# Giving the normalising transposes a stretch of their own, with the scores ahead of the maxima behind it

## The chip, the cores and the metric

The kernel runs on one core of one Trainium2 chip. The metric is the device time of one execution in microseconds (us); the time before is the median of three runs. Everything that is read out of a profile comes from one profiled execution, whose own time stands beside it.

## What is computed

A sequence of 2048 rows of 640 numbers passes through four residual layers, A, B, A, B. Each layer first normalises its input rows. A is a linear attention block, B an attention block over four segments of 512 rows with a causal softmax inside a segment and a memory that carries over from the segments before. Both have 32 heads of 20 columns. Cut to what matters:

```python
def _A_ref(x, wqkv, wo):
    q, k, v = split_heads(x @ wqkv)
    phi = lambda t: jnp.where(t > 0, t + 1, jnp.exp(t)) + 1e-6
    pq, pk = phi(q), phi(k)
    kv = einsum("bhsd,bhse->bhde", pk, v)
    o = (pq @ kv) / (pq . sum(pk))
    return merge(o) @ wo

def _B_ref(x, wq, wk, wv, wo, beta):
    for s in range(4):
        logits = einsum("bhqd,bhkd->bhqk", qs, ks) * scale + causal_mask
        a_dot = softmax(logits) @ vs
        a_mem = (phi(qs) @ M) / (phi(qs) . z)
        o = g * a_mem + (1 - g) * a_dot
        M, z = M + phi(ks)^T vs, z + sum(phi(ks))
    return merge(o) @ wo

x = x + _A_ref(_layernorm(x), A...)
x = x + _B_ref(_layernorm(x), B...)
x = x + _A_ref(_layernorm(x), A...)
x = x + _B_ref(_layernorm(x), B...)
```

The change touches only the softmax part of B: scores, their row maxima, the exponentials, the weighted sum and the division by the sum.

## The kernel before, in words

Two generators write the program. One (`dense`, line 893) issues all projections, transposes and memory reads; the other (`attention`, line 799) issues the softmax part of B. `run` (line 972) interleaves them: each step of a generator returns a cost in nanoseconds, and the generator whose running cost is lower goes next (the dense costs are first divided by a rate that depends on the phase). TensorE (PE) executes in exactly the order in which the program is written. For the other engines a scheduler decides the order when the program is built, and it also decides which of the eight PSUM banks each result gets: all PSUM results share one pool of eight banks (`bank`, line 137), and a matmul that opens a bank waits until the engine that reads the bank's previous content is done.

The softmax part works on groups: a group is four heads of one segment, 8 groups to a segment, 32 to a B layer, 64 in all. A group has a pair index p (0, 1), a parity (0, 1) and row blocks of 128. Three groups are in flight, called new, prev and old, and one pass over a group's turn is a cycle. The operations of a cycle stand in the table `STRETCHES` (line 54), cut into three stretches; after each stretch `attention` gives up its turn at a cost of `SLOT` = 2420 (line 836), so that dense work goes between the stretches. An entry is an operation, an index and the group that it is for (0 new, 1 prev, 2 old):

- `max` (`row_max`, line 692): scores of query rows against keys, four or six matmuls (line 701) into two banks; VectorE (DVE) reads each bank with a masked maximum (line 708). Entries 0 to 3 have six matmuls or a pair of 512 columns with it, entry 4 has four of 256 columns.
- `split` and `rows` (lines 712 and 722): the maxima are split into two halves on DVE (lines 717 and 718), turned by one transpose on PE (line 726), copied by ScalarE (ACT, line 728) and sent by DMA into two rows of the query tile (line 731), so that the next score matmul subtracts the maximum itself.
- `exp` (`scores`, line 734): transposed scores, matmuls at line 743; each bank is read by one exponential on ACT (line 747), and GpSimd (POOL) clears what the mask excludes (line 754). Entries 0 and 1 open four banks in all, entries 2 and 3 four, entry 4 two.
- `sum` (`weigh`, line 762): the weighted sum, 16 matmuls (line 770; the profile counts 32 rows, since each runs as two) into one bank.
- `copy` (`evacuate`, line 774): ACT copies that bank to SBUF as `oTf` (line 776).
- `out` (`normalize`, line 778): the normalising transposes, four on PE from `oTf` into one bank (line 783); DVE takes the reciprocals of the sums (`rc`, line 786) and multiplies (line 790 for a first segment, otherwise `tmp`, line 793); POOL adds `tmp` to the output (line 794).

Before, a cycle on PE was therefore: scores of entry 4, maxima 0 and 1, the row transpose, the weighted sum, the copy on ACT; dense work; the transposes, maxima 2 and 3, scores 0 and 1; dense work; scores 2 and 3, maximum 4; dense work. The middle stretch opened nine banks: one for the transposes, four for maxima, four for scores.

A dense piece is 15 matmuls into one bank (line 337 with 320 columns or line 323 with 512; the latter is written as 9 and 6 around a turn), two or three transposes (line 280), three matmuls of a memory read (line 382), or four transposes or matmuls of the memory update (lines 589 and 597). Its bank is read by ACT (line 360, 404, 561, 349, 351 or 284) or by DVE.

Of the kernel before, what the change touches and what calls it, by code (L numbers as in the profile page):

```python
# [38 lines left out]
VW = H * E1 + 11  # L39
HB = H // 2  # L40
COL = 1 / 2.4
SLOT = 2420.0
R_SECOND, R_PROJ, R_MID, R_END = 2.2, 1.0, 1.2, 0.85


# [5 lines left out]
EXPS += [[((0, a, 2, 0), (1, a, 2, 256)) for a in range(2)]]  # L51


STRETCHES = [[("exp", 4, 2), ("max", 0, 0), ("max", 1, 0), ("rows", 0, 1), ("sum", 0, 2), ("sum", 1, 2), ("sum", 3, 2),
              ("sum", 2, 2), ("copy", 0, 2)],
             [("out", 0, 2), ("max", 2, 0), ("max", 3, 0), ("exp", 0, 1), ("exp", 1, 1)],
             [("exp", 2, 1), ("exp", 3, 1), ("max", 4, 0), ("split", 0, 0), ("load", 0, 0)]]


def constants():  # L60
# [64 lines left out]
class Kernel:  # L125
# [673 lines left out]
    def attention(self, segs):  # L799

        prev = old = ahead = None
        n = 0
        while n < NSEG * NG or prev or old:
            new = None
            if n < NSEG * NG:
                st = segs[n // NG]
                if not st.get("projected"):
                    yield lambda: st.get("projected")
                new = ahead or self.stacks(st, n % NG)
                ahead = None  # L810
            n += 1
            for stretch in STRETCHES:
                for op, k, back in stretch:
                    G = (new, prev, old)[back]
                    if op == "load" and n < NSEG * NG and segs[n // NG].get("projected"):
                        ahead = self.stacks(segs[n // NG], n % NG)
                    if G is None:
                        continue
                    if op == "max":
                        self.row_max(G, MAXES[k])  # L820
                    elif op == "split":
                        self.split_max(G)
                    elif op == "rows":
                        self.max_rows(G)
                    elif op == "exp":
                        for bank in EXPS[k]:
                            self.scores(G, bank)
                    elif op == "sum":
                        self.weigh(G, k)
                    elif op == "copy":  # L830
                        self.evacuate(G)
                    elif op == "out":
                        if not G["st"].get("remembered"):
                            yield lambda: G["st"].get("remembered")
                        self.normalize(G)
                yield SLOT
            old, prev = prev, new


# [188 lines left out]
```

## Time and profile before

| | us |
|---|---|
| median of three runs | 1817.21 (1815.69 to 1820.99) |
| the profiled execution | 1820.7 |
| its span, first to last instruction | 1818.9 |
| PE busy in the span | 1716.8 (94%) |
| DVE busy | 1112.6 (61%) |
| ACT busy | 940.2 (52%) |
| POOL busy | 549.1 (30%) |

A line of the profile names the source line, the engine, the operation and the tiles (`out<-in`), with how many instructions it holds; times are in us, means in ns. PEld is the loading of weights, which runs beside the matmuls. `<-` in a wait names what ended the idle time. The table of waits has the total, the number of waits and the longest. The timeline merges neighbouring instructions of one kind into a row: start, length, engine and line, and in square brackets the idle time ahead of it. The matmuls are pipelined and their ends are modelled, so the length of a row of matmuls runs on past the start of the next.

### The profile page before, as it was taken

Reading aid. Unit: us, or ns where it says so; the run is one execution under the profiler, and the core shown is the slowest. Engines: PE = TensorE matmul, PEld = TensorE weight load, DVE = VectorE, ACT = ScalarE, POOL = GpSimd, SP = SyncE. Lnnn points to the kernel's source line nnn. Section 1 sums busy time; section 2 is a strip of 40 time slices with the busy share of each in tenths; the row PEclk is TensorE's granted clock in tenths of the full one; section 3 lists DMA queues with packets and bytes.
Section 4 is the critical chain, followed back from the end, with each engine's and each line's share of the span. In section 5 each row is a group of like instructions: output and inputs, shape, how many; then the busy total and the mean of one; then the engine's idle time right before and its main releaser. Section 6 shows DMA issues by size and latency. Waiting matters only on the chain.

```text
span 1818.9 us, 36252 instructions
## 1 busy us (share of the span) xinstructions
PE 1716.8 (94%) x13032; PEld 1068.9 (59%) x13032; DVE 1112.6 (61%) x3729; ACT 940.2 (52%) x1753; POOL 549.1 (30%) x981
## 2 busy tenths in 40 slices
PE   6999999999999999998989999999999999999998
PEld 4666676654665565453556776756546546644555
DVE  7655443677777677766662321527677777777773
ACT  5455433266556546655564433223664664565664
POOL 1534440022123213324355334200221231232442
PEclk9999999999999999999999999999999999999999
DMA  7443343312212332352212112433122223223332
GB/s 256 155 166 116 147 144 100 122 53 93 94 63 85 109 100 72 109 195 66 72 56 89 51 34 91 138 100 101 50 92 90 92 85 103 96 77 107 127 109 88
DMA packets 123371, 185.96 MB, mean 102 GB/s; under 512 B 13740, under 2 KB 85548, under 8 KB 121016
## 3 DMA queue, kind: packets, MB, share of 16 engines
q1 hardware_dynamic: 109480, 137.44, 23.5%
q0 software_dynamic: 4496, 25.23, 3.8%
q10 hardware_dynamic: 9216, 20.98, 2.9%
q8 instruction: 103, 1.69, 0.4%
q14 instruction: 76, 0.62, 0.1%
HBM read 104.41 MB, written 78.64 MB: 101 GB/s over the span
## 4 chain that ended last, share of the span: by engine, by line
PE 75%; DVE 11%; ACT 5%; issue 4%; POOL 2%; DMA 2%; SPq 1%; ACTq 0%; POOLq 0%; DVEq 0%
PE ps L337 32%; PE ps L323 18%; PE ps L770 7%; DVE junk L708 4%; PE ps L743 3%; PE ps L280 3%; PE ps L382 3%; ACT pe L747 2%; PE ps L701 2%; PE ps L467 2%; PE ps L597 1%; POOL e L353 1%; PE ps L783 1%; DVE st L298 1%; DMA qs<-mt 1%
## 5 line engine op out<-in xcount | busy, mean ns | idle before, releaser
L708 DVE CUSTOM_DVE_ANT_0 junk<-ps,maskw 128x512 bf16<-128x512 f32 (+3 forms) x1024 | 499.5, 488 | 90.2 <-PE ps L701 28.7
L747 ACT ACTIVATE pe<-ps,lsc 128x512 f32<-128x512 f32 x640 | 391.7, 691 | 124.0 <-PE ps L743 116.9
L754 POOL TENSOR_SCALAR_AFFINE_SELECT pe<-pe 128x256 f32<-128x256 f32 (+1 forms) x640 | 232.0, 369 | 426.3 <-ACT pe L747 420.1
L337 PEld LDWEIGHTS <-xT 128*128 128x128 f16 x2880 | 281.5, 99 | 123.1 <-issue 9.2
L337 PEld LDWEIGHTS <-oT 128*128 128x128 f16 x1920 | 186.9, 98 | 80.3 <-issue 6.0
L353 POOL TENSOR_SCALAR e<-e 128x320 f32<-128x320 f32 (+1 forms) x104 | 163.6, 1573 | 160.8 <-ACT e L349 153.3
L770 PE MATMUL ps<-pe,v 128*32 128x512 f32 (+3 forms) x2048 | 155.9, 439 | 13.1 <-ACT pe L747 5.9
L743 PE MATMUL ps<-qs,ks 62*128 62x512 f16 (+3 forms) x1024 | 132.4, 299 | 24.1 <-DVE mg L708 12.1
L337 PE MATMUL ps<-w_Bo,oT 128*128 128x320 f16 x960 | 142.2, 301 | 2.9 <-ACT oT L284 1.2
L337 PE MATMUL ps<-w_Av,xT 128*128 128x320 f16 x960 | 142.0, 306 | 1.1 <-DVE w_Av L246 1.0
L337 PE MATMUL ps<-w_Bv,xT 128*128 128x320 f16 x960 | 141.6, 301 | 0.1
L323 PE MATMUL ps<-xT,w_Bq 128*128 128x512 f16 x600 | 140.7, 382 | 0.4 <-ACT pe L747 0.2
L337 PE MATMUL ps<-w_Ao,oT 128*128 128x320 f16 x960 | 139.5, 299 | 0.0
L323 PE MATMUL ps<-xT,w_Bk 128*128 128x512 f16 x600 | 139.5, 379 | 0.0
L323 PE MATMUL ps<-xT,w_Aq 128*128 128x512 f16 x600 | 136.0, 379 | 0.9 <-DVE xT L285 0.5
L337 PE MATMUL ps<-w_Ak,xT 128*128 128x320 f16 x960 | 135.6, 299 | 0.6 <-DVE tmp L793 0.6
L360 ACT ACTIVATE v<-ps 128x320 f32<-128x320 f32 x128 | 55.4, 435 | 128.5 <-PE ps L337 124.2
L303 POOL TENSOR_TENSOR rs<-rs,mhalf 128x1 f32<-128x1 f32 x64 | 35.5, 555 | 282.8 <-DVE rs L302 282.8
L701 PE MATMUL ps<-ks,qs 60*128 60x512 f16 (+3 forms) x1024 | 110.1, 298 | 7.4 <-ACT pe L747 4.7
L770 PEld LDWEIGHTS ps<-pe,v 128*32 128x32 f32 x2048 | 64.8, 110 | 82.7 <-issue 67.4
L562 DVE SCALAR_TENSOR_TENSOR nat<-ps,nat 128x512 f16<-128x512 f32 x80 | 55.2, 690 | 95.1 <-ACT nat L561 93.0
L323 PEld LDWEIGHTS <-w_Bq 128*128 128x128 f16 x600 | 57.2, 99 | 71.2 <-issue 9.7
(156 smaller groups left out, 2268.1 us busy)
## 6 DMA issues: line engine op xcount, KB each, us to landing
x<-xn ACTq DMA_DIRECT2D x48, 320.0 KB
qs<-qd SPq DMA_DIRECT2D x128, 120.0 KB
ks<-kd SPq DMA_DIRECT2D x128, 120.0 KB
xo<-x SPq DMA_DIRECT2D x48, 320.0 KB
pqd<-pq POOLq DMA_DIRECT2D x40, 256.0 KB, 2.4
pqi<-pqd SPq DMA_DIRECT2D x32, 320.0 KB
qd<-nat SPq DMA_DIRECT2D x40, 256.0 KB
kd<-nat SPq DMA_DIRECT2D x40, 256.0 KB
```

What stands on the lines that cost most here:

```text
L280: nc.tensor.transpose(pt[:, (c - c0) * P:(c - c0 + 1) * P], src[:, c * P:(c + 1) * P], self.ident)
L323: nc.tensor.matmul(p, w[:, c, a, t * P:(t + 1) * P], xT[:, c, b, :], start=k == 0, stop=k == 3 * C - 1)
L337: nc.tensor.matmul(p, xT[:, c, a, i * P:(i + 1) * P], w[:, c, b, n * HN:(n + 1) * HN], start=k == 0, stop=k == 3 * C - 1)
L353: nc.gpsimd.tensor_scalar(e, e, 1.0, eps, op0=OP.min, op1=OP.add)
L360: self.nc.scalar.activation(vv[:, n * HB:(n + 1) * HB, :DH], p.rearrange("p (h e) -> p h e", e=DH), AF.Copy, scale=V_SHIFT)
L562: nc.vector.scalar_tensor_tensor(nat[:, 1], p, QK_SHIFT, nat[:, 0], op0=OP.mult, op1=OP.subtract)
L701: nc.tensor.matmul(bs[par][:, a:a + n], qs[r, p, i * P:(i + 1) * P], ks[r, p, :n], start=True, stop=True)
L708: nc.vector.tensor_tensor_reduce(junk[:, :n], bs[par][:, a:a + n], self.maskw[:, SEG - n:], 1.0, NEG, OP.add, OP.max, G["mg"][:, par, p, i ...
L743: nc.tensor.matmul(b[:, a:a + n], ks[r, p, j * P:(j + 1) * P], qs[r, p, j * P:], start=True, stop=True)
L747: nc.scalar.activation(e, b, AF.Exp, scale=self.lsc)
L754: nc.gpsimd.affine_select(d, d, pattern=pat, compare_op=OP.is_ge, fill=0.0, base=0, channel_multiplier=-1)
L770: nc.tensor.matmul(G["pv"][32 * h4:32 * h4 + 32, j * P:], v[j][:, h * E1:h * E1 + 32], G.pop((p, par, j)), start=j == 0, stop=j == 2, skip ...
```

## The change

The table of stretches now carries a cost per stretch instead of one constant. The transposes leave the middle stretch and become a stretch with one entry, 1220 in cost; the stretch ahead of them falls from 2420 to 1200, so that a cycle still adds up to 7260. In the stretch behind, scores 0 and 1 now stand ahead of maxima 2 and 3. It opens eight banks.

```diff
-SLOT = 2420.0
...
-STRETCHES = [[("exp", 4, 2), ("max", 0, 0), ("max", 1, 0), ("rows", 0, 1), ("sum", 0, 2), ("sum", 1, 2), ("sum", 3, 2),
-              ("sum", 2, 2), ("copy", 0, 2)],
-             [("out", 0, 2), ("max", 2, 0), ("max", 3, 0), ("exp", 0, 1), ("exp", 1, 1)],
-             [("exp", 2, 1), ("exp", 3, 1), ("max", 4, 0), ("split", 0, 0), ("load", 0, 0)]]
+
+STRETCHES = [(1200.0, [("exp", 4, 2), ("max", 0, 0), ("max", 1, 0), ("rows", 0, 1), ("sum", 0, 2), ("sum", 1, 2),
+                       ("sum", 3, 2), ("sum", 2, 2), ("copy", 0, 2)]),
+             (1220.0, [("out", 0, 2)]),
+             (2420.0, [("exp", 0, 1), ("exp", 1, 1), ("max", 2, 0), ("max", 3, 0)]),
+             (2420.0, [("exp", 2, 1), ("exp", 3, 1), ("max", 4, 0), ("split", 0, 0), ("load", 0, 0)])]
...
-            for stretch in STRETCHES:
+            for slot, stretch in STRETCHES:
...
-                yield SLOT
+                yield slot
```

The file grows by one line, so that line 743 of before is line 744 of after, and so on. Each piece below is of the same cycle, the one that starts at 1442.82 us in the trace of before.

On PE, from the end of the weighted sum (L770, then L771) to the scores. Before:

```order
L770 MATMUL ps<-pe,v_84 32x256 x4
L337 LDWEIGHTS xT
L337 MATMUL ps<-w_Bv,xT 128x320
...
L783 MATMUL ps<-ident,oTf 128x128 x4
L701 LDWEIGHTS qs
L701 MATMUL ps<-ks_2753,qs 128x512
...
L743 LDWEIGHTS ks_2752
L743 MATMUL ps<-qs,ks_2752 128x512
```

After:

```order
L771 MATMUL ps<-pe,v_84 32x256 x4
L784 MATMUL ps<-ident,oTf 128x128 x4
L338 LDWEIGHTS xT
L338 MATMUL ps<-w_Bv,xT 128x320
...
L744 LDWEIGHTS ks_2752
L744 MATMUL ps<-qs,ks_2752 128x512
...
L702 LDWEIGHTS qs
L702 MATMUL ps<-ks_2753,qs 128x512
```

The transposes moved from behind the dense piece to directly behind the weighted sum, and the scores from behind the maxima to directly behind the dense piece. In 21 of the 63 cycles that have all three the transposes follow the weighted sum with nothing between them, where before a dense piece stood between them in every one; in four more, one short piece stands there (two transposes of line 280 in two of them, the four transposes of line 589 in the other two).

On DVE, in the same cycle, from the reciprocals to the second maximum. Before:

```order
L786 RECIPROCAL rc_18159<-ps 128x16
L708 ISA junk,mg<-ps,maskw 128x512
L708 ISA mg 128x1
L793 TENSOR_TENSOR tmp<-ps,rc_18159 128x320
L708 ISA junk,mg<-ps,maskw 128x512
```

After:

```order
L787 RECIPROCAL rc_18140<-ps 128x16
L794 TENSOR_TENSOR tmp<-ps,rc_18140 128x320
L709 ISA junk,mg<-ps,maskw 128x512
L709 ISA mg 128x1
L709 ISA junk,mg<-ps,maskw 128x512
```

A masked maximum no longer stands between the reciprocal and the product that empties the transposes' bank.

On ACT the order in this cycle is the same in both; of after (L777 copies the weighted sum, L361 reads a dense piece, L748 are the exponentials):

```order
L777 ACTIVATE oTf<-ps,cg 128x512
L361 ACTIVATE v_80<-ps 128x16x20
L748 ACTIVATE pe<-ps,lsc 128x512 x4
L361 ACTIVATE v_81<-ps 128x16x20
L748 ACTIVATE pe<-ps,lsc 128x512 x4
```

The copy of the dense piece still stands ahead of the four exponentials; the dense piece itself now ends where the scores begin. The banks moved too. In the middle stretch of before, the fourth score took over the bank of the first maximum and the next dense piece the bank of the transposes in this cycle. In after, the first bank that is opened behind the four scores and two of the maxima or more is that of the first score: in 27 of 62 cycles a dense piece behind the stretch opens it, and in 35 it is already the last maxima's bank.

## The prediction

> **What bounds the kernel now.** I read the page first.
>
> ```profile
> span 1818.9 us, 36252 instructions
> PE 1716.8 (94%) x13032; PEld 1068.9 (59%) x13032; DVE 1112.6 (61%) x3729; ACT 940.2 (52%) x1753; POOL 549.1 (30%) x981
> ```
>
> PE carries the kernel; DVE and ACT are far from full on average, so what counts is where PE stands still for one of them. The profiled execution took 1820.7 us, 1.8 us of it outside the span; it is 3.5 us above the median of 1817.2. I make the sum against the profiled execution and carry the difference over to the median. The table of waits comes next.
>
> ```profile
> PEld L743 <- DVE tmp L793: 19.5, 18, 1.6
> PE ps L743 <- DVE mg L708: 12.1, 23, 0.9
> PEld L337 <- DVE tmp L793: 7.8, 7, 1.8
> PEld L743 <- DVE otok L790: 7.7, 10, 1.0
> PEld L726 <- DVE m L718: 15.7, 31, 1.5
> ACT oTf L776 <- PE ps L770: 87.7, 56, 3.5
> ```
>
> The first four rows, 47.1 us, are scores and dense pieces that wait for a bank which DVE still reads: the bank of the transposes or of a maximum. They belong to the middle stretch, and the change goes for them. How such a wait comes about, one cycle of the timeline shows, the one whose order is printed above.
>
> ```profile
> 1442.58 0.68 DVE L708 CUSTOM_DVE_ANT_0 junk<-ps,maskw 128x512 bf16<-128x512 f32 x1
> 1442.82 2.36 PE L770 MATMUL ps<-pe,v 128*32 128x512 f32 x32
> 1445.12 2.21 PE L337 MATMUL ps<-w_Bv,xT 128*128 128x320 f16 x15
> 1445.30 0.69 ACT L776 ACTIVATE oTf<-ps,cg 128x512 f32<-128x512 f32 x1 [1.50 <-PE ps L770]
> 1445.91 0.29 DVE L708 CUSTOM_DVE_ANT_0 junk<-ps,maskw 128x128 bf16<-128x128 f32 x1
> 1447.16 0.60 PE L783 MATMUL ps<-ident,oTf 128*128 128x128 f32 x4
> 1447.36 0.44 ACT L360 ACTIVATE v<-ps 128x320 f32<-128x320 f32 x1 [1.38 <-PE ps L337]
> 1447.70 0.61 PE L701 MATMUL ps<-ks,qs 60*128 60x512 f16 x6
> 1447.80 0.26 DVE L786 RECIPROCAL rc<-ps 128x16 f32<-128x16 f32 x1 [1.59 <-PE ps L783]
> 1448.12 0.69 DVE L708 CUSTOM_DVE_ANT_0 junk<-ps,maskw 128x512 bf16<-128x512 f32 x1
> 1448.14 1.11 PE L743 MATMUL ps<-qs,ks 62*128 62x512 f16 x4
> 1448.62 2.42 ACT L747 ACTIVATE pe<-ps,lsc 128x512 f32<-128x512 f32 x4 [0.81 <-PE ps L743]
> 1448.74 0.49 DVE L793 TENSOR_TENSOR tmp<-ps,rc 128x320 f32<-128x320 f32 x1
> 1449.28 2.21 PE L337 MATMUL ps<-w_Bv,xT 128*128 128x320 f16 x15
> 1451.42 0.61 PE L743 MATMUL ps<-qs,ks 62*128 62x384 f16 x8
> 1451.62 0.29 DVE L708 CUSTOM_DVE_ANT_0 junk<-ps,maskw 128x128 bf16<-128x128 f32 x1
> 1451.87 0.39 PE L701 MATMUL ps<-ks,qs 60*128 60x256 f16 x4
> 1452.19 2.21 PE L337 MATMUL ps<-w_Bv,xT 128*128 128x320 f16 x15
> 1452.29 0.42 DVE L708 CUSTOM_DVE_ANT_0 junk<-ps,maskw 128x256 bf16<-128x256 f32 x1 [0.37 <-PE ps L701]
> 1454.47 0.35 DVE L718 SCALAR_TENSOR_TENSOR m<-mg,m 128x16 f16<-128x16 f32 x1
> 1455.09 0.23 PE L726 MATMUL pm<-ident,m 128*32 128x128 f16 x1
> ```
>
> I read starts, not lengths. The six matmuls of the maxima run from 1447.70 to 1448.14, 0.44 us for 2 x 1024 columns. The four scores have as many columns, yet from their start to the next dense piece it is 1449.28 - 1448.14 = 1.14 us: 0.70 us is waiting. The end of it is `tmp`, 1448.74 + 0.49 = 1449.23, which empties the transposes' bank; the piece starts 0.05 us later.
>
> The Trainium skill says in "Perfetto Trace Analysis", Identifying the Most-Contended Engine, that matmul busy time is no good measure, because matmuls are pipelined. The trace agrees: these four scores show as 1.11 us busy. By the waits alone the place is worth 47 us, by starts 60 us (next paragraph); I take the starts.
>
> There are 64 such groups of scores. From the start of each to the start of what follows on PE they take 88.2 us together; the first and the last are:
>
> ```profile
> 371.83 0.38 PE L743 MATMUL ps<-qs,ks 62*128 62x512 f16 x2
> 374.28 0.76 PE L280 MATMUL ps<-ident,xh 128*128 128x128 f32 x5 [0.51 <-ACT pe L747]
> ...
> 1783.65 0.60 PE L743 MATMUL ps<-qs,ks 62*128 62x512 f16 x4
> 1784.18 0.44 PE L280 MATMUL ps<-ident,otok 128*128 128x128 f32 x2
> 1784.45 2.20 PE L337 MATMUL ps<-w_Bo,oT 128*128 128x320 f16 x15
> ```
>
> At 0.44 us of work each, 28.2 us, 60 us of the 88.2 are waiting. That is all that the change can win in this place.
>
> **The change part by part.** No instruction is added or removed; PE, DVE, ACT, POOL and the queues do the same work in another order. POOL's addition of `tmp` and the DMAs of the row maxima keep their places within the cycle, and I cost them at nothing: POOL has 70% of the span free.
>
> *What goes.* With `tmp` directly behind `rc`, the transposes a dense piece ahead and eight banks in the stretch, the wait for the transposes' bank and the first maximum goes: 60 us, in whole, because every one of these banks is now opened later than its reader ends.
>
> *The transposes wait for the copy.* Where nothing stands between the weighted sum and the transposes, PE waits for ACT. In the cycle shown the copy ends at 1445.30 + 0.69 = 1445.99; PE was free at 1445.12. The transposes then start 0.05 us later, as the dense piece did behind `tmp`, and with their weights to load first perhaps 0.15: I take 1.0 us. ACT is idle 1.50 us ahead of this copy, and 87.7 us over 56 cycles, so that it starts at once as a rule. 21 cycles x 1.0 and four with a short piece between x 0.55 (0.27 us or 0.49 us of it covered) make 23 us; the ends are 20 and 27. Queued behind the transposes on PE are the dense piece, the scores and the maxima, and so DVE's next work too.
>
> *The bank of the first score.* What is late next is the first exponential. In the cycle shown it starts 1448.62 - 1448.14 = 0.48 us behind the first score, and with 0.69 us for one (row below) it is over at 1.17; a piece that takes its bank starts at 1.22. PE has done scores and maxima at 0.88. So even with ACT free there is a wait of 0.33 us. ACT is often not free: the dense piece now ends where the scores begin, and its copy starts 0.20 us later (1447.36 - 1447.16) and takes 0.44 or 0.53 us, ahead of the exponentials: 0.16 to 0.25 us more. Where the piece is read by the split of a projection (0.60 us), it is 0.32 more. And where the next piece is short, two transposes of 0.27 us (1784.45 - 1784.18), the piece behind waits again for the second exponential, which ends 0.58 us after the first ((2.42 - 0.69) / 3).
>
> ```profile
> L747 ACT ACTIVATE pe<-ps,lsc 128x512 f32<-128x512 f32 x640 | 391.7, 691 | 124.0 <-PE ps L743 116.9 <-PE ps L701 2.9 <-POOL otok L794 2.3
> L404 ACT ACTIVATE xn<-ps,ioB 128x320 f32<-128x320 f32 x56 | 29.7, 530 | 48.3 <-PE ps L337 47.9
> L561 ACT ACTIVATE nat<-ps 128x512 f16<-128x512 f32 x80 | 47.9, 599 | 98.5 <-PE ps L323 64.8 <-issue 27.7 <-PE ps L701 1.9
> ```
>
> By these numbers I went through the built order cycle by cycle. In 27 cycles the first bank of a dense piece is that of the first score: 0.33 to 0.94 us, 0.68 in the mean, 18 us. In 35 cycles the last maximum already has that bank, opened 0.67 us behind the first score: 0.56 to 1.36 us with the piece behind it, 0.96 in the mean, 34 us. Together 52 us; the ends are 62 x 0.33 = 20 us (the copies don't matter and no second piece waits) and 62 us.
>
> *The maxima come later.* They start 0.44 us later behind the same point, and DVE's chain from them to the row transpose follows: four banks of maxima take 3.62 us (1442.58 to 1446.20), then the last maxima to the split 2.53 us (1452.29 to 1454.82). In the cycle shown the split was done 0.27 us ahead of the transpose at 1455.09. `tmp` leaves this chain, which takes about 0.2 us off it (3.62 + 0.43 against 1447.70 to 1451.91 = 4.21). About 25 cycles have this little dense work and no slack to spare; at 0.3 us that is 7 us. Its ends are 0 and 0.45 x 62 = 28 us. Where the stretch behind is short, the bank of the last maximum is still being read when the next piece wants it: six cycles by 0.5 us, 3 us.
>
> *The exponentials come earlier* relative to DVE by the 0.44 us. Later waits for ACT should shrink: I count 16 us of waiting at the last maxima and 36 at the row transpose, from starts as above, most of it named as DVE's (the `m` row), so that I take 5 us off, with ends of 0 and 26.
>
> *The cycle shown, replayed.* Weighted sum 0 to 2.30; transposes 3.3 to 3.84; dense piece to 5.88; scores and maxima to 6.76; first exponential over at 5.88 + 0.64 + 0.69 = 7.21, the next piece at 7.26 and to 9.40; eight scores and the last maxima to 10.17; dense piece to 12.31; row transpose 0.76 later at 13.07. DVE: maxima from 6.74 to 10.36, last maxima and split to 12.9, in time. The next weighted sum comes at 13.1 instead of 12.28. A cycle with a dense piece ahead of its transposes wins 0.2 us instead: the wait of 0.70 becomes one of 0.50.
>
> *Sum:* -60 + 23 + 52 + 7 + 3 - 5 = +20 us: 1840.7 against the profiled execution, 1837 against the median of 1817.2.
>
> **The rivals.** *Eight banks suffice.* "Perfetto Trace Analysis", Identifying Performance Opportunities, in the Trainium skill says that consistent bubbles on the busiest engine can mean that there isn't enough PSUM for the next tile. The trace agrees, with these banks. The mechanism here would be that a stretch of eight banks fits the pool, and the wait for the first score's bank doesn't come about either: -60 + 23 = -37, or 1780 us. It decides if the first exponential is over within 0.88 us of the first score; the 1.17 us above speaks against it. Chance 0.06.
>
> *Only the first exponential counts* (faster). If ACT is free at the scores and the second exponential is never waited for, the bank term is 20 us, not 52: -60 + 23 + 20 + 7 + 3 - 5 = -12, or 1805 us. Point of decision: a mean wait behind the scores and maxima below 0.5 us. For it speaks ACT's 52%; against it that the built order puts the dense copy ahead of the exponentials. Chance 0.14.
>
> *The head start is paid back* (no change). If the exponentials' lead takes 26 us off the later waits instead of 5, the sum is -1: 1816 us. Against it: the waits there are named as DVE's. Chance 0.12.
>
> *DVE's chain becomes the bound* (slower still). If the 0.45 us by which the maxima start later reach the row transpose in every cycle, the 7 becomes 28: +41, or 1858 us. For it speaks that the split was only 0.27 us ahead in a dense cycle; against it that many cycles have more dense work. Chance 0.11.
>
> **How the numbers follow.** My forecast has 0.57: 1837 us. Faster by over 0.3% (5.5 us, about what a measurement of this kernel can tell from no change) has 0.06 + 0.14 = 0.20, within it 0.12, slower 0.57 + 0.11 = 0.68. The range takes in the bank-term rival's 1805 below, and above 1853: the forecast with its bank term at 62, the copy wait at 27 and 2 us more of DVE. It leaves out the first rival and most of the last, 0.15. Slower cases alone, which hold most of the chance, lie between 1823 and 1853.
>
> **What would show it.** In the profile of after: a new wait of PE's weight loads at L784 for the copy at L777, about 21 times 0.9 us; PE waits for L748 behind scores and maxima, on dense lines and on L702; the waits for `tmp` gone from the first dozen; the span of the cycle that starts at 1442.82 before longer by 0.8 us. The forecast is wrong if the time from the first score to the piece behind the maxima is 0.9 us in most cycles (then the first or second rival), or if the row transpose waits for `m` much longer than 15.7 us (then the last).

## The result and the profile after

The changed kernel takes 1829.62 us (median of four runs, 1827.54 to 1834.53) against 1816.99 for before, a ratio of 1.0064 with a 95% interval of 1.0044 to 1.0085: slower by 11.6 us, between 8.0 and 15.4. The forecast was 20 slower, with a range from 1805 to 1853 us. The profiled execution took 1834.5 us, the highest of its four, as that of before was the highest of its own; the two spans differ by 13.8 us.

The head of the page shows the same work: the same number of instructions on each of the five engines, busy times within 3.3 us. (The total in the first line is 48 lower than in before; the counts in the second line are the same.)

```profile
span 1832.7 us, 36204 instructions
PE 1713.5 (93%) x13032; PEld 1069.4 (58%) x13032; DVE 1112.3 (61%) x3729; ACT 941.1 (51%) x1753; POOL 551.8 (30%) x981
```

In the table of waits (after's lines are one higher than before's) stand the rows that answer to those shown of before:

```profile
PEld L702 <- DVE tmp L794: 3.7, 7, 0.7
PEld ps L784 <- ACT oTf L777: 31.8, 26, 1.4
PE ps L784 <- ACT oTf L777: 20.2, 26, 0.9
PE ps L702 <- ACT pe L748: 14.1, 42, 0.8
PEld ps L281 <- ACT pe L748: 12.9, 27, 0.9
PE ps L281 <- ACT pe L748: 5.4, 22, 0.6
PEld L727 <- DVE m L719: 16.3, 34, 1.5
```

The four rows of scores and dense pieces that waited 47 us for `tmp` and other banks of DVE are gone; 3.7 us of waiting for `tmp` are left at the maxima. New are the transposes, which wait for the copy of the weighted sum, and the last maxima and dense transposes, which wait for an exponential. The two rows of line 784 show the same waiting once for the weights and once for the matmul, so that they are not to be added; their 26 waits are the 22 below and the four cycles with one short piece between. The row transpose's wait for `m` is as before (15.7).

As in the prediction, starts say more than lengths. I took each group of matmuls from its start to the start of the next group on PE, subtracted the time that such a group takes where nothing holds it up, and added the rest by kind of passage. This is worked out from all matmuls of both traces, from 340 us on:

| passage on PE | before, us | after, us | forecast of the difference |
|---|---|---|---|
| scores 0, 1 to the dense piece | 60.0 | 0.2 | -60 |
| weighted sum to transposes | 0 | 24.5 (22 times) | +23 |
| maxima 2, 3 to the piece behind | 6.0 | 43.3 | +52 |
| maximum 4 to the piece behind | 16.3 | 22.4 | +3 |
| last maxima, row transpose, weighted sum | 37.0 | 36.5 | +7 - 5 |
| everything else | 58.6 | 65.8 | 0 |
| together | 177.9 | 192.7 | +20 |

The row of maxima 2, 3 holds in both columns also the passage behind maxima 0 and 1 in the first cycle of each B layer, where nothing else of the softmax follows yet: 1.45 us each, 2.9 us together, in before and in after alike.

The cycle that the prediction replayed starts in after at 1449.57. From the timeline, its rows on PE, ACT and DVE from the end of the weighted sum on:

```profile
1452.04 0.69 ACT L777 ACTIVATE oTf<-ps,cg 128x512 f32<-128x512 f32 x1 [1.40 <-PE ps L771]
1452.78 0.66 PE L784 MATMUL ps<-ident,oTf 128*128 128x128 f32 x4 [0.86 <-ACT oTf L777]
1453.28 2.20 PE L338 MATMUL ps<-w_Bv,xT 128*128 128x320 f16 x15
1453.47 0.26 DVE L787 RECIPROCAL rc<-ps 128x16 f32<-128x16 f32 x1 [0.45 <-PE ps L784]
1453.77 0.49 DVE L794 TENSOR_TENSOR tmp<-ps,rc 128x320 f32<-128x320 f32 x1
1455.41 0.60 PE L744 MATMUL ps<-qs,ks 62*128 62x512 f16 x4
1455.51 0.44 ACT L361 ACTIVATE v<-ps 128x320 f32<-128x320 f32 x1 [2.79 <-PE ps L338]
1455.85 0.60 PE L702 MATMUL ps<-ks,qs 60*128 60x512 f16 x6
1455.89 2.42 ACT L748 ACTIVATE pe<-ps,lsc 128x512 f32<-128x512 f32 x4
1456.27 0.69 DVE L709 CUSTOM_DVE_ANT_0 junk<-ps,maskw 128x512 bf16<-128x512 f32 x1 [2.01 <-PE ps L702]
1456.63 2.20 PE L338 MATMUL ps<-w_Bv,xT 128*128 128x320 f16 x15 [0.18 <-ACT pe L748]
1462.45 0.23 PE L727 MATMUL pm<-ident,m 128*32 128x128 f16 x1
```

The transposes come 0.05 us after the copy's end, 3.21 us after the weighted sum's start (replayed: 3.3). `tmp` is done 1.15 us before the scores want their banks. The dense piece behind the maxima starts 1456.63 - 1455.41 = 1.22 us behind the first score, and ACT's first exponential ended at 1455.89 + 0.69 = 1456.58: the 1.22 us that the prediction gave for a free ACT, where PE had work for 0.88. (Its replay of this cycle had 1.38, with the dense copy ahead of the exponentials.) The cycle lasts 12.99 us, against 12.28 before and 13.1 in the replay.

### The profile page after: what moved, and what is told of

It reads as the page before. It is cut to its first block, busy times and chain, and to the rows that moved or that the text cites. A ratio compares the mean times of both kernels' runs of the same rounds, so it can differ in the third digit from the quotient of the medians.

```text
span 1832.7 us, 36204 instructions
## 1 busy us (share of the span) xinstructions
PE 1713.5 (93%) x13032; PEld 1069.4 (58%) x13032; DVE 1112.3 (61%) x3729; ACT 941.1 (51%) x1753; POOL 551.8 (30%) x981
## 4 chain that ended last, share of the span: by engine, by line
PE 73%; DVE 11%; ACT 7%; issue 4%; POOL 3%; DMA 2%; SPq 0%; ACTq 0%; DVEq 0%; POOLq 0%
PE ps L338 31%; PE ps L324 17%; PE ps L771 8%; DVE junk L709 4%; ACT pe L748 4%; PE ps L383 3%; PE ps L281 3%; PE ps L744 3%; PE ps L468 2%; PE ps L702 2%; PE ps L784 2%; PE ps L598 1%; POOL e L354 1%; DVE st L299 1%; ACT oTf L777 1%
## 5 line engine op out<-in xcount | busy, mean ns | idle before, releaser
L748 ACT ACTIVATE pe<-ps,lsc 128x512 f32<-128x512 f32 x640 | 393.1, 691 | 101.7 <-PE ps L744 95.7
L771 PE MATMUL ps<-pe,v 128*32 128x512 f32 (+3 forms) x2048 | 158.9, 446 | 11.3 <-ACT pe L748 3.7
L702 PE MATMUL ps<-ks,qs 60*128 60x512 f16 (+3 forms) x1024 | 124.3, 297 | 20.7 <-ACT pe L748 14.1
L361 ACT ACTIVATE v<-ps 128x320 f32<-128x320 f32 x128 | 55.4, 435 | 135.9 <-PE ps L338 132.1
L771 PEld LDWEIGHTS ps<-pe,v 128*32 128x32 f32 x2048 | 65.7, 112 | 81.6 <-issue 67.8
L744 PE MATMUL ps<-qs,ks 62*128 62x384 f16 (+3 forms) x1024 | 105.8, 300 | 4.5 <-DMA qs<-mt 3.2
L562 ACT ACTIVATE nat<-ps 128x512 f16<-128x512 f32 x80 | 47.9, 599 | 104.4 <-PE ps L324 72.3
```

The lines of the kernel that those rows point to most:

```text
L361: self.nc.scalar.activation(vv[:, n * HB:(n + 1) * HB, :DH], p.rearrange("p (h e) -> p h e", e=DH), AF.Copy, scale=V_SHIFT)
L702: nc.tensor.matmul(bs[par][:, a:a + n], qs[r, p, i * P:(i + 1) * P], ks[r, p, :n], start=True, stop=True)
L744: nc.tensor.matmul(b[:, a:a + n], ks[r, p, j * P:(j + 1) * P], qs[r, p, j * P:], start=True, stop=True)
L748: nc.scalar.activation(e, b, AF.Exp, scale=self.lsc)
L771: nc.tensor.matmul(G["pv"][32 * h4:32 * h4 + 32, j * P:], v[j][:, h * E1:h * E1 + 32], G.pop((p, par, j)), start=j == 0, stop=j == 2, skip ...
```

## The experiments

Each ratio is against runs of before on the same chip; the medians of before there were 1817.35 us for the first four kernels, 1819.38 for the next four (from `seven_maxima` on) and 1818.91 for the last four (from `short_exp` on). The sums of waiting by passage are made as in the table above. Where the expectations say 39 and 44 us for the wait behind maxima 2 and 3, they leave out the first cycles of the two B layers; counted as here it is 40 and 47 us, and the text adds the first cycles. Where a kernel is compared with the change by their two ratios, the difference has an error of some 4 us, from the two intervals. Line numbers are those of before in `split_only`, those of after in the kernels made from after with nothing but a shortened read, and one below before's where there are three stretches.

**Only the new stretch.** `split_only` is the change with scores and maxima back in the old order.

```diff
-             (2420.0, [("exp", 0, 1), ("exp", 1, 1), ("max", 2, 0), ("max", 3, 0)]),
+             (2420.0, [("max", 2, 0), ("max", 3, 0), ("exp", 0, 1), ("exp", 1, 1)]),
```

> The transposes keep the stretch of their own, but the maxima stand ahead of the scores again, as before. Theory (three terms add up): the 60 us of waiting behind the four scores stay away, the copy wait of about 24 us (21 cycles, 0.92 to 0.97 us each) stays, and the wait of 37 us for the bank of the first score, with the 8 us of the pieces behind it, falls to about 10, because the bank that the dense piece opens is now that of the first maximum: -60 + 24 + 10 = -26 against before, about 1791 us, and about 38 us faster than the change. Rival (the split of the stretch is what costs, the order inside is indifferent): within 5 us of the change, 1825 to 1835. Second rival (waits are conserved: what goes in one place comes back in another because ACT or DVE sets the length of a cycle): 1812 to 1825.

Measured: 1831.86 us, ratio 1.0080 (1.0066 to 1.0093), 14.5 us slower than before. The theory missed by 41 us; the first rival holds. The copy wait is there as expected, 25.2 us in 22 cycles, but the wait behind the scores is still 44.2 us, not 10. The timeline of the same cycle shows why:

```profile
1453.60 0.61 PE L701 MATMUL ps<-ks,qs 60*128 60x512 f16 x6
1454.03 0.69 DVE L708 CUSTOM_DVE_ANT_0 junk<-ps,maskw 128x512 bf16<-128x512 f32 x1 [1.57 <-PE ps L701]
1454.05 0.60 PE L743 MATMUL ps<-qs,ks 62*128 62x512 f16 x4
1454.78 1.52 PE L337 MATMUL ps<-w_Bv,xT 128*128 128x320 f16 x10
```

The first maximum starts 0.43 us behind its matmul and takes 0.69 us. It ends at 1454.72, and the dense piece starts at 1454.78, 1.18 us behind the first matmul of the stretch. With the scores first it was 1.22. DVE's first reader is no quicker than ACT's: in this cycle a stretch of eight banks waits in either order. In 20 of the 62 cycles the piece behind starts at this 1.18 us, and in four at 1.32, where the first maximum itself starts 0.15 us later; in the others it is longer. So the 60 us do not go because the transposes leave; without the change of order 44 of them stay.

**Only the order.** `swap_only` has the transposes in the middle stretch again, and scores ahead of maxima; the diff is against before.

```diff
-             [("out", 0, 2), ("max", 2, 0), ("max", 3, 0), ("exp", 0, 1), ("exp", 1, 1)],
+             [("out", 0, 2), ("exp", 0, 1), ("exp", 1, 1), ("max", 2, 0), ("max", 3, 0)],
```

> The transposes go back to the middle stretch, directly ahead of the scores, and the scores stay ahead of the maxima. Theory: no copy wait (a dense piece stands between the weighted sum and the transposes), the wait for the first score's bank stays at 37 us and 8 behind it, and some 4 us come in for the last maximum's bank, which is that of the transposes: -60 + 0 + 45 + 4 = -11 against before, about 1806 us, and 23 us faster than the change. Rival (the order of scores and maxima is the whole loss, through DVE's later maxima): 1825 to 1835. Second rival (waits are conserved): 1812 to 1825.

Measured: 1816.21 us, ratio 0.9992 (0.9982 to 1.0003), no change against before, and 13 us faster than the change (1.0064 less 0.9992, of 1817). That is what the second rival gave. The waits are:

```profile
PEld L700 <- DVE tmp L792: 20.6, 36, 1.3
PE ps L700 <- ACT pe L746: 16.9, 39, 1.1
PEld L725 <- DVE m L717: 17.1, 35, 1.8
```

The transposes wait for no copy (0 us), the maxima wait again for `tmp` and for the exponentials. By passages the middle stretch has 48.4 us behind the maxima (with one of the two first cycles; the other lies ahead of 340 us here), where before had, counted alike, 60.0 behind the scores and 4.5 behind the maxima; against this gain of 16 stand 6 more between the first maxima and the row transpose (30.2 against 24.5 us), 7 more behind maximum 4 (23.4 against 16.3) and small ones. Both orders come out at the same time here. The kernel before, `swap_only`, `split_only` and the change are the four combinations of the two edits: the new stretch costs 14.5 us with the maxima first (1.0080) and 13 with the scores first (1.0064 less 0.9992), and the order is worth 1.5 us without the new stretch and 3 with it, neither clear of the error.

**The transposes a whole stretch later.** In `late_scores` and `late_maxima` they head the last stretch, so that two dense pieces and eight banks lie between the copy and them; the two differ in the order of scores and maxima.

```diff
-             (1220.0, [("out", 0, 2)]),
...
-             (2420.0, [("exp", 2, 1), ("exp", 3, 1), ("max", 4, 0), ("split", 0, 0), ("load", 0, 0)])]
+             (2420.0, [("out", 0, 2), ("exp", 2, 1), ("exp", 3, 1), ("max", 4, 0), ("split", 0, 0), ("load", 0, 0)])]
```

(and 2420 for the first stretch, so that a cycle's cost stays 7260.)

> The transposes go to the front of the last stretch, so that a dense piece, eight banks and another dense piece lie between the copy and them; scores ahead of maxima. Theory: the copy wait goes, the wait for the first score's bank stays: -60 + 45 = -15 against before, about 1802 us. Rival (DVE's chain to the row transpose becomes the bound, since reciprocal and product now stand between the four banks of maxima and the last maxima): the waits at the row transpose grow from 18 us by 20 or more, 1815 or slower.

> The transposes at the front of the last stretch as in the run before this one, and the maxima ahead of the scores as in before. Theory: neither the copy wait nor the wait for the first score's bank: -60 + 10 = -50 against before, about 1767 us, 35 us faster than with the scores first. Rival (DVE's chain becomes the bound): the gain is taken at the row transpose, 1800 or slower. Second rival (waits are conserved): 1810 to 1825.

Measured: 1831.02 us, ratio 1.0075 (1.0058 to 1.0092), with the scores first; 1822.78, ratio 1.0034 (1.0021 to 1.0046), with the maxima first. Both theories missed, by 29 and 56 us. In the first, the copy wait is gone and the wait behind the maxima is 48.8 us, but the rival's mechanism is not seen either: the wait ahead of the row transpose is 27.1 us against 24.5. What grew are waits inside the last stretch (scores 2, 3 to maximum 4: 12.7 against 3.3; behind maximum 4: 24.0 against 16.3) and small ones on dense pieces. So a kernel without the copy wait is not faster for that alone: where the transposes stand matters too. In the second the wait behind the scores is 42.8 us, as in `split_only`; its time lies where both of its rivals had put it, though the first rival's longer wait at the row transpose is not there. Its profiled execution was 1.3 us below its median and that of before 3.5 above, so the passages don't account for the last 6 us; that stays open.

**Fewer banks in the stretch.** `seven_maxima` takes before and moves two of the four scores of the middle stretch to the last, which then opens eight banks; `seven_scores` does it with the scores first; `seven_early` puts the last maxima and their split ahead of the scores there as well. The stretches of the three, in this order:

```diff
+[("out", 0, 2), ("max", 2, 0), ("max", 3, 0), ("exp", 0, 1)]
+[("exp", 1, 1), ("exp", 2, 1), ("exp", 3, 1), ("max", 4, 0), ("split", 0, 0), ("load", 0, 0)]
...
+[("out", 0, 2), ("exp", 0, 1), ("max", 2, 0), ("max", 3, 0)]
+[("exp", 1, 1), ("exp", 2, 1), ("exp", 3, 1), ("max", 4, 0), ("split", 0, 0), ("load", 0, 0)]
...
+[("out", 0, 2), ("exp", 0, 1), ("max", 2, 0), ("max", 3, 0)]
+[("max", 4, 0), ("split", 0, 0), ("exp", 1, 1), ("exp", 2, 1), ("exp", 3, 1), ("load", 0, 0)]
```

> The order of before (transposes, maxima, scores in one stretch), but two of the four score banks go over to the last stretch, which then opens eight banks; the middle one opens seven. Theory A (the wait behind the stretch is there because the next dense piece must take a bank that the stretch itself has just filled): the 60 us behind the scores fall below 15, the last stretch gains up to 15: -30 against before, about 1787 us. Theory B (a wait of PE that is taken away comes back behind it, since the same readers must empty the same banks in the same cycle): the waits behind the last stretch and at the row transpose grow by most of it, 1810 to 1822.

> The same, with the two score banks that stay in the middle stretch ahead of the maxima. Theory A: the 44 us behind the maxima that the run with the transposes put back showed fall below 12, the last stretch gains up to 15: about 1795 us. Theory B: 1810 to 1822. If the order of scores and maxima in the stretch matters, this run and the one with the maxima first differ by over 6 us; if it doesn't, they agree.

> As the run before this one, but in the last stretch the last maxima and their split stand ahead of the scores, so that DVE's chain to the row transpose starts 0.7 us earlier. If that chain is what sets the cycle, the waits at the row transpose (24 us behind the maxima 0 and 1, 12 behind the transpose) fall by 20 or more and the time with them; if ACT is (the exponentials come 0.3 us later), the time stays or rises by 5 to 10 us.

Measured: 1838.48 us, ratio 1.0100 (1.0082 to 1.0117); 1845.28, ratio 1.0137 (1.0117 to 1.0157); 1859.08, ratio 1.0215 (1.0195 to 1.0234). All three are slower than either theory gave. Half of theory A is right: the wait behind the middle stretch falls from 60.0 to 18.3 us, and with the scores first from 48.4 in `swap_only` to some 20. But the banks are only filled elsewhere. In `seven_maxima` the last stretch waits 38 us between its scores and maximum 4, against 3.3 before; in `seven_early` 91 us stand behind its scores, against 16.3 us behind that stretch before, and its scores wait twice as long for a maximum's bank as the 12.1 us of before:

```profile
PE ps L742 <- DVE mg L707: 24.3, 47, 1.1
```

Moving the split forward took the named wait for `m` at the row transpose to 2.8 us, from 22.8 in before (15.7 for its weights and 7.1 for the matmul) and 14.0 in `seven_scores`. But the passage ahead of it still holds 24.5 us, as in before, with other releasers, and the time rose by 14 us. So an earlier split does not help these kernels. That the banks make them slow is what the places of the waits suggest; no run changed the banks alone. The scores first cost 7 us here, just over the 6 that were to tell whether the order matters.

**The row transpose.** `rows_later` is before with one entry moved.

```diff
-("max", 1, 0), ("rows", 0, 1), ("sum", 0, 2), ("sum", 1, 2),
+("max", 1, 0), ("sum", 0, 2), ("rows", 0, 1), ("sum", 1, 2),
```

> Before, with one thing changed: the row transpose stands behind the first quarter of the weighted sum instead of ahead of it, 0.9 us later, so that the split is done when PE comes to it. Theory A (each wait stands for itself): the 24 us at the row transpose fall below 6, -18, about 1799 us, unless the rows' DMA then comes late for the scores. Theory B (waits come back): the 60 us behind the scores or the 16 behind the last stretch grow by most of it, 1812 to 1819.

Measured: 1804.85 us, ratio 0.9921 (0.9906 to 0.9936), 14.4 us faster than before. Theory A is the nearer one, 6 us off: the weight load's wait for `m` goes from 15.7 to 7.3 us, and that of the matmul from 7.1 to 0.6. The matmul's row of before, and then the rows of `rows_later`:

```profile
PE pm L726 <- DVE m L718: 7.1, 10, 1.2
```

```profile
PEld L725 <- DVE m L717: 7.3, 12, 1.5
PE pm L725 <- DVE m L717: 0.6, 1, 0.6
PE ps L769 <- DVE rc L388: 5.2, 1, 5.2
PE ps L769 <- ACT r L350: 3.1, 7, 0.7
```

By passages the waits ahead of and behind the row transpose and behind the weighted sum fall from 44.7 to 35.4 us, and another 5 us go between dense pieces. Of the 35.4, 20.5 stand in a new place, between the maxima and the weighted sum that now follows them directly. In 42 of the 60 cycles that is under 0.1 us; the rest are 18 waits, the longest of which is for DVE (`rc` of a memory read), while seven are for ACT's reading of a dense piece (`r`). Why the weighted sum gets a bank that these still hold stays open. The wait behind the scores is 60.2, untouched. So waits are not always handed on.

**The two new waits, shortened.** Both kernels are the change with one read cut to 128 columns; the rest of what it should read is left out, and in `short_exp` POOL fills the gap, 64 more instructions of 0.42 us. On PE all 13032 rows keep their order in `short_copy`, and all but two neighbours in `short_exp`. `short_exp` cuts the first exponential of each middle stretch, `short_copy` the copy of the weighted sum.

```diff
-        nc.scalar.activation(e, b, AF.Exp, scale=self.lsc)
+        w, _ = (P, nc.gpsimd.memset(e[:, P:], 0.5)) if todo is EXPS[0][0] else (512, 0); nc.scalar.activation(e[:, :w], b[:, :w], AF.Exp, scale=self.lsc)
```

> The changed kernel, with the first exponential of every stretch of eight banks cut to its first 128 of 512 columns (the rest of its tile is filled with 0.5 by POOL, so the softmax is computed from wrong numbers). By the slope between ACT's copies of 320 and 512 columns (435 and 690 ns) it takes about 0.18 us instead of 0.69. Theory (the wait behind the maxima is for the first scores' banks): the 39 us of it fall to about 10, and the time by 18 to 28 us against the change, about 1807 us. Rival (the stretch's wait is set by all its readers together, of which this is one in eight, or by DVE): the wait stays above 30, and the time within 6 us of the change.

```diff
-        self.nc.scalar.activation(G["oT"], G["pv"], AF.Copy, scale=self.cg[:, G["g"]:G["g"] + 1])
+        self.nc.scalar.activation(G["oT"][:, :P], G["pv"][:, :P], AF.Copy, scale=self.cg[:, G["g"]:G["g"] + 1])
...
-            nc.tensor.transpose(pt[:, i * P:(i + 1) * P], oT[:, i * P:(i + 1) * P], self.ident)
+            nc.tensor.transpose(pt[:, i * P:(i + 1) * P], oT[:, :P], self.ident)
```

> The changed kernel, with ACT's copy of the weighted sum cut to 128 of 512 columns, which all four transposes then read (the output is wrong). Theory (the transposes behind the weighted sum wait for this copy, and a wait there is worth its length): the 24.5 us fall by 22 x 0.5 = 11 to about 13, the time by 11, to about 1818 us. Rival (such a wait is partly handed on: banks and rows that come later are then ready): the 11 us of waiting go, but the time falls by 7 or less.

The groups by form show what was cut, first the exponentials in `short_exp`, then the copy in `short_copy`; the waits behind them are those of `short_copy` for the copy:

```profile
L748 ACT ACTIVATE pe<-ps,lsc 128x512 f32<-128x512 f32 x576 | 355.7, 691 | 31.7 <-PE ps L744 28.2 <-PE ps L702 2.9 <-PE ps L281 0.5
L748 ACT ACTIVATE pe<-ps,lsc 128x128 f32<-128x128 f32 x64 | 23.3, 365 | 70.8 <-PE ps L744 67.3 <-POOL otok L795 3.1
```

```profile
L777 ACT ACTIVATE oTf<-ps,cg 128x128 f32<-128x128 f32 x64 | 23.4, 366 | 86.2 <-PE ps L771 86.1
```

```profile
PEld ps L784 <- ACT oTf L777: 23.2, 24, 1.1
PE ps L784 <- ACT oTf L777: 12.0, 23, 0.6
```

Each instruction became 0.32 to 0.33 us shorter, not the 0.51 that I had expected. `short_exp`: 1822.11 us, ratio 1.0019 (1.0008 to 1.0030), against the change's 1.0064 a gain of 0.45% or 8 us; the wait behind the maxima falls by 14.2 to 29.1 us, of 62 x 0.33 = 20 that the shorter instruction could give. So the first score's exponential sets much of this wait, though the fall to 10 us did not come. How much of the 14 reached the end stays open: the ratios say 8, with an error of some 4, the spans of the two profiled executions differ by 12.0 us, and behind maximum 4 there are 4.0 us more. `short_copy`: 1822.62 us, ratio 1.0017 (1.0006 to 1.0029), a gain of 8.5 us; the copy wait falls from 24.5 to 17.4 us, which is 22 x 0.32 = 7.0, and the time falls by no less, within the same error of 4. The rival's bound of 7 us lies within that error, so the two can't be told apart by it, but nothing of the wait is seen to come back.

**Two edits together.** `after_rows` is the change with the row transpose moved, `swap_rows` is `swap_only` with it.

> The changed kernel, with the row transpose behind the first quarter of the weighted sum, which made before 14.5 us faster. If that gain stands by itself: -14, about 1815 us. If the change has already used the slack (the row transposes of the changed kernel wait 36 us, as in before): no other sum; a gain below 8 would say that the wait for the first score's bank grows instead.

> The transposes in the middle stretch, scores ahead of maxima, and the row transpose behind the first quarter of the weighted sum: the change without its copy wait, with the best edit so far. Adding what the single edits gave (-1 and -14): about 1803 us, level with the row transpose alone moved. If scores ahead of maxima are worth something once DVE's chain has slack: below 1800.

Measured: 1824.40 us, ratio 1.0031 (1.0020 to 1.0042), 6 us faster than the change; and 1814.86, ratio 0.9978 (0.9963 to 0.9992), 4 us faster than before. Neither is the sum of its parts. In `after_rows` the waits ahead of the row transpose go, but the copy wait rises from 24.5 to 27.6 and the one behind the maxima from 43.3 to 47.1. In `swap_rows` the latter is 53.5 us, and 11.5 us stand between transposes and scores, against 8 in `swap_only`. With the same place of the row transpose, the scores first are now 10 us slower than the maxima first (0.9978 against 0.9921). The best kernel of all is `rows_later`, which leaves the order of the middle stretch alone: it beats both.

## Why the prediction was right, and where it was not

- *-60, the waits behind the scores:* 60.0 us became 0.2, to the place. But the reason given, that the banks come free because the transposes leave and `tmp` comes sooner, carries only 16 of the 60 (`split_only`: 44.2). The rest went because the scores no longer stand last: the wait moved with the place behind the stretch, from the scores to the maxima. The -60 and the +52 were not two effects of two edits but mostly one wait under two names. That the term fits to the place is luck.
- *+23, the copy wait:* 24.5 us in 22 cycles against 21 x 1.0 and four short ones; 19 of the 22 are 0.87 to 1.0 us, three are 1.3 to 3.1. That it counts in the time is shown by `short_copy`, which shortens the copy and keeps PE's order: 7 us less of it make the kernel 8.5 faster. A dense piece between makes the change 13 us faster (`swap_only`, with the bank waits some 6 us longer and the row transpose's 4), and the new stretch costs as much in either order. So this wait makes up much of the loss, but the place of the transposes has a share too: `late_scores` has no copy wait and is no faster than the change. A kernel that keeps the new stretch and always has a piece between was not run.
- *+52, the bank of the first score:* the mechanism and its 1.22 us are in the trace, the term is too large: 43.3 us behind the maxima, 37 more than before. The step that failed is "ahead of the exponentials: 0.16 to 0.25 us more" for a dense copy of 0.44 us. In the cycle shown the copy starts 0.10 us behind the first score and ends at 1455.95, 0.06 us after the first exponential's start in the record: it costs nothing, for the exponential starts 0.48 us behind the first score, as in before, where ACT was idle. Over the 62 cycles it starts at 0.42 to 0.49 us in 45, at 0.53 in eight, at 0.60 to 0.65 in seven and later in two. The waits behind the maxima gather at 0.34 to 0.38 us (22 of 62), 0.6 to 0.68 (20) and 0.9 to 1.1 (14); my mean was 0.84, the measured 0.65. Where the last maxima do not wait themselves (24 cycles) it is 0.36 against my 0.68, where they do (38) 0.83 against 0.96.
- *+3, the last maximum's bank:* 6.1 us, twice the term.
- *+7 - 5, the chain to the row transpose:* -0.5 us. Neither the later maxima nor the earlier exponentials show there; whether they cancel stays open. The rival that made this chain the bound is out: its wait stayed at 16 us.
- *Left out:* 7 us of small waits, 2 of them between a dense piece and the transposes and most of the rest at the start of the stretch, ahead of the scores.
- *The rivals:* eight banks did not suffice, and the mean wait behind scores and maxima, 0.65 us, lies above the 0.5 at which the second would have held. The head start was not paid back: the last maxima's wait grew.
- *The sum:* right in sign, 8 us too high against the ratio's 11.6 and 5 against the waits' 14.8. The bank term alone is 15 too high; the small waits left out (7) and the last maximum's bank (3) made up most of that, which is luck too.

## What to carry to other kernels

When a stretch fills every bank that there is, the work behind it waits for the stretch's first reader, whichever engine that is: in the cycle shown 1.18 us with DVE first and 1.22 with ACT first, against 0.88 us of matmuls. Changing the order gives the wait another name; look for how much time lies between the first fill and the next taker before costing a wait as gone. And a chain of two dependent operations on PE with another engine's copy between them needs work between them: here it cost 0.9 to 1.0 us nearly each time that a table of costs let the two meet, and moving one small waiting transpose (the row transpose, behind a quarter of the next group) was worth more, 14.4 us, than all of the reordering, none of which made the kernel faster.

## What the runs showed of the hardware that was not expected

ACT's time for an exponential from PSUM is 365 ns for 128 columns and 691 for 512: 0.85 ns a column and, by the line through these two, some 256 ns that do not depend on the length. The copies agree (366 against 686 ns). Taking the slope from two different copies (435 ns for 320 columns, 690 for 512) had made the shortened instruction 0.18 us. The line gives 528 ns for 320 columns, and the copy of line 404, shown in the prediction, takes 530; it is the copy of 435 ns that lies off it, for a reason that no run looked into.
